# Attention on one core: one query block's scores of heads 1 to 13 made once and kept in SBUF, the maxima subtracted there by GpSimd

## The chip, the core and the metric

The kernel runs on one core of a Trainium2 chip. The core has a matrix engine (TensorE, "PE" in the profile, with its weight loads as "PEld"), a vector engine (DVE), a scalar engine for activation functions (ACT), GpSimd (POOL) and an engine that here issues DMAs (SP). Each runs its own list of instructions in order, and waits for the others through semaphores. SBUF is the on-chip memory that all of them use; matmuls write to PSUM, eight banks of 128 x 512 f32, from which DVE and ACT read. The metric is the time of one execution on the device in microseconds (us).

## The reference

A transformer block on 2048 tokens of width 448, all in f32:

```python
h = _layernorm(x) * (1 + ca) + sa            # ca, sa, ga, ... from silu(c) @ w_mod
q, k, v = heads(h @ wqkv)                    # 16 heads of 28
p = softmax(q @ k.T * 28 ** -0.5)            # 2048 x 2048 for each head
x = x + ga * (merge(p @ v) @ wo)
h = _layernorm(x) * (1 + cb) + sb
z = gelu(h @ w_in); z1, z2 = z[:, :896], _layernorm(z[:, 896:])
x = x + gb * ((z1 * (w_sp @ z2 + b_sp)) @ w_out)
```

The change is in the second and third of these lines' softmax. Everything behind it (the projection with `wo` and the gated MLP) is computed as before.

## The kernel before, in words

**Three stages.** The first 145 us make q, k and v (q and k are split into a high and a low part and go through DRAM to be stacked by head). The attention follows, to 864 us. The rest is the MLP, in which PE multiplies a combined form of `w_sp` whose block sums GpSimd has made during the attention.

**Scores are made twice.** The maximum of each query over all keys must be known before the exponential. For head h, `kst[h % 3]` and `qst[h % 3]` hold the stacked keys and queries, 128 rows x 2048. `m_mm` (PE L728) multiplies 128 queries by 512 keys into PSUM, queries on the partitions, and DVE takes the maximum along the keys (L733). That is 64 matmuls and 64 reductions a head. `m_max` then gathers them on DVE (L740) and negates and splits them on GpSimd (L742 to L143), `m_fin` transposes them on PE (L749), DVE copies them (L751), and two DMAs put them into rows 84 and 85 of `qst`, where `kst` has rows of ones. From then on every product of `kst` and `qst` has the query's maximum subtracted already. `s_mm` (PE L760) makes the scores a second time, now 128 keys by 512 queries, keys on the partitions; ACT takes the exponential out of PSUM into a tile `P` (L764), and `pv_mm` (PE L775) multiplies `V` by `P` into one PSUM bank for the whole head. A unit `u` is one key tile of 128 of one head: four `s_mm`, one for each block `qb` of 512 queries, and their exponentials. There are 256 units, 16 a head.

**What sets the order.** The schedule is written out by hand: the order in which the Python code issues is the order on each engine. The loop goes over units. In unit `u` it alternates the four `s_mm` of `u` with the four `m_mm` of unit `u + LEAD`, LEAD = 20, so that a head's maxima are ready when its exponentials start. After every second unit the products with `V` of the last two are issued. Other work is hung on slots (a slot is a unit's number) in two tables, `events` ahead of the unit and `late` behind it: the loading of a head's keys and queries (`load_head`, 30 slots ahead of the head), `m_max` and `m_fin` four slots ahead of it, the normalisation of the head before (`n_copy`, `n_sum`, `n_recip`, `n_bcast`, `n_mul`, `n_scatter`, at slots 1 to 9 of the next head), and on GpSimd the sums and differences of blocks of `w_sp` (`W_SUMS`, `ws_op`, slots 2 to 200; L882 adds or subtracts, L877 negates), whose blocks SP loads and stores in the same order. SP's list is in order too: a store waits there for the GpSimd operation ahead of it, and whatever stands behind waits with it.

**Buffers.** Seven PSUM banks serve scores and maxima; which of them a matmul gets is fixed when the program is written, by `First`, a small table of assumed times in units of one matmul. `P` has six tiles for two exponentials each. Two large SBUF areas that held the normed input of the first stage (`heapD0`, `heapD1`) and one that held the weights for q and k (`heapD2`) serve as the place of the attention's output `OT` and of the prepared `wo`.

## Time and profile before

| | |
|---|---|
| median of 3 runs (lowest to highest) | 1375.57 us (1374.93 to 1377.33) |
| span of the profiled execution, first to last instruction | 1375.3 us |
| busy over the span: PE, PEld, DVE, ACT, POOL | 1370.1, 973.9, 1069.3, 789.5, 356.1 us |
| granted TensorE clock | 1.000 |
| attention, first to last product with V | 150.9 to 863.5 us |

The span is what the profile shows of one execution, and it is 0.2 us from the median of the timed runs, so sums over the profile can be set against the median without a correction. "Busy" is the time in which at least one instruction of an engine was under way. PE's matmuls overlap, so PE counts as busy even where it goes from one matmul to the next more slowly than it could; for what one matmul costs, the distance from start to start is the thing to read. POOL's spans are rough.

### The profile page before, as it was taken

To read this page: it belongs to the slowest core of one execution; us is meant where nothing else is said; L and a number is where in the kernel's file an instruction comes from. 1 tells how busy PE (TensorE), PEld (TensorE's weight loads), DVE (VectorE), ACT (ScalarE), POOL (GpSimd) and SP (SyncE) were. 2 spreads that over 40 slices of the span, in tenths; PEclk is the share of its full clock that TensorE was granted. 3 is DMA by queue.
4 is the path that set the end of the run, shared out by engine and by line. 5 is a ranking of instruction groups with operands and counts; after the bars stand their busy time and mean duration, and the time that the engine had idled before them with its cause. 6 is when DMAs were issued, how large, how long until landed. Compare 5 with 4: busy or idle time off the path is not lost.

```text
span 1375.3 us, 20071 instructions
## 1 busy us (share of the span) xinstructions
PE 1370.1 (100%) x7088; PEld 973.9 (71%) x7088; DVE 1069.3 (78%) x1729; ACT 789.5 (57%) x1466; POOL 356.1 (26%) x358
## 2 busy tenths in 40 slices
PE   9999999999999999999999999999999999999998
PEld 8888655555555555555555554888898888888898
DVE  8898888888888888888888880662268798889682
ACT  6623666676767676767777779364234754444221
POOL 2144334243335544633442302200142000000000
PEclk9999999999999999999999999999999999999999
DMA  8464642455244534552343321533202433335842
GB/s 296 138 177 176 187 118 85 109 161 153 69 117 138 151 121 124 156 148 77 110 126 88 96 57 50 174 142 126 85 1 77 130 100 115 115 93 180 270 158 83
DMA packets 93345, 174.65 MB, mean 127 GB/s; under 512 B 17016, under 2 KB 32250, under 8 KB 90698
## 3 DMA queue, kind: packets, MB, share of 16 engines
q1 hardware_dynamic: 90526, 169.07, 40.9%
q10 hardware_dynamic: 2718, 4.30, 0.9%
q8 instruction: 56, 0.92, 0.3%
q14 instruction: 45, 0.37, 0.1%
HBM read 111.71 MB, written 56.82 MB: 123 GB/s over the span
## 4 chain that ended last, share of the span: by engine, by line
PE 97%; DVE 1%; ACT 0%; issue 0%; DMA 0%; POOL 0%; DVEq 0%; ACTq 0%
PE st_ps L760 19%; PE acc L1442 19%; PE o_ps L775 17%; PE mt L728 17%; PE z_ps L1334 5%; PE z_ps L1166 5%; PE pq L415 4%; PE wo_ps L1031 3%; PE y_ps L1522 2%; PE y_ps L1521 2%; PE y_ps L1520 2%; PE pv L397 2%; PE tp L193 1%; DVE st L368 0%; PE pv L554 0%
## 5 line engine op out<-in xcount | busy, mean ns | idle before, releaser
L733 DVE TENSOR_REDUCE pm<-mt 128x1 f32<-128x512 f32 x1024 | 631.3, 682 | 85.9 <-PE mt L728 85.8
L764 ACT ACTIVATE P<-st_ps 128x512 f32<-128x512 f32 x1024 | 514.4, 630 | 201.8 <-PE st_ps L760 201.8
L760 PE MATMUL st_ps<-qst,kst 128*128 128x512 f32 x1024 | 404.3, 406 | 0.0
L728 PE MATMUL mt<-kst,qst 128*128 128x512 f32 x1024 | 402.5, 393 | 0.1
L760 PEld LDWEIGHTS st_ps<-qst,kst 128*128 128x128 f32 x1024 | 191.2, 188 | 141.4 <-issue 93.1
L775 PE MATMUL o_ps<-P,V 128*32 128x512 f32 x2048 | 247.1, 598 | 0.0
L1442 PE MATMUL acc<-wsp_h,heapA 128*128 128x512 f32 x752 | 231.5, 389 | 0.0
L728 PEld LDWEIGHTS mt<-kst,qst 128*128 128x128 f32 x1024 | 192.4, 188 | 32.0 <-POOL kst L665 0.5
L882 POOL TENSOR_TENSOR ws_raw<-ws_raw 128x512 f32<-128x512 f32 x124 | 159.3, 1288 | 195.7 <-DMA ws_scr<-ws_raw 138.9
L1442 PEld LDWEIGHTS acc<-wsp_h,heapA 128*128 128x128 f32 x752 | 141.1, 188 | 29.2
L1442 PE MATMUL acc<-wsp_l,heapA 128*128 128x512 f32 x376 | 146.3, 389 | 0.0
L775 PEld LDWEIGHTS o_ps<-P,V 128*32 128x32 f32 x2048 | 54.7, 109 | 122.9 <-issue 114.6
L1222 ACT ACTIVATE wsp_h<-raw_sp 128x512 fp32r<-128x512 f32 x104 | 65.6, 632 | 125.7 <-PE acc L1442 111.2
L143 DVE TENSOR_TENSOR wsp_l<-raw_sp,wsp_h 128x512 fp32r<-128x512 f32 x104 | 70.4, 687 | 16.6 <-ACT wsp_h L1222 16.4
L1442 PEld LDWEIGHTS acc<-wsp_l,heapA 128*128 128x128 f32 x376 | 70.6, 188 | 14.7
L415 PE MATMUL pq<-heapD,heapD 128*128 128x512 f32 x196 | 61.8, 390 | 0.0
L1338 DVE BATCH_NORM_STATS2 stz<-z 128x6 f32<-128x448 f32 x32 | 19.9, 626 | 44.6 <-ACT z L1337 44.5
L143 DVE TENSOR_TENSOR heapA<-z,heapA 128x1536 fp32r<-128x1536 f32 (+2 forms) x25 | 39.9, 1605 | 6.6 <-ACT heapA L1257 6.5
L1337 ACT ACTIVATE z<-z_ps 128x448 f32<-128x448 f32 x32 | 17.4, 543 | 47.4 <-PE z_ps L1334 47.4
L415 PEld LDWEIGHTS pq<-heapD,heapD 128*128 128x128 f32 x196 | 36.7, 188 | 7.4
L804 POOL TENSOR_TENSOR osb<-osb,rb 128x512 f32<-128x512 f32 x15 | 19.3, 1287 | 85.6 <-DMA rb<-r_scr 80.8
L1521 PE MATMUL y_ps<-wouts,uT 128*128 128x448 f32 x112 | 40.9, 365 | 0.0
(231 smaller groups left out, 1432.1 us busy)
## 6 DMA issues: line engine op xcount, KB each, us to landing
ws_scr<-ws_raw SPq DMA_DIRECT2D x92, 256.0 KB
raw_sp<-ws_scr SPq DMA_DIRECT2D x92, 256.0 KB
ws_raw<-in_w_spT_dram SPq DMA_DIRECT2D x72, 256.0 KB
kst<-qk_scr SPq DMA_DIRECT2D x45, 224.0 KB
qst<-qk_scr SPq DMA_DIRECT2D x45, 224.0 KB
qk_scr<-qh SPq DMA_DIRECT2D x28, 256.0 KB
qk_scr<-ql SPq DMA_DIRECT2D x28, 256.0 KB
z_scr<-z1t SPq DMA_DIRECT2D x28, 256.0 KB
```

The lines of the kernel that those rows point to most:

```text
L143: eng.tensor_tensor(out=dst, in0=a, in1=hi.bitcast(F32), op=ALU.subtract)
L415: pe.matmul(pq, wqk[:, b, m * 128 : (m + 1) * 128], hT[g][:, a, :], start=j == 0, stop=j == NST - 1)
L728: pe.matmul(mt, qst[h % 3][:, t * 128 : (t + 1) * 128], kst[h % 3][:, kb * 512 : (kb + 1) * 512], start=True, stop=True)
L733: dve.tensor_reduce(out=pms[h][:, t, kb : kb + 1], in_=mt, axis=AX.X, op=ALU.max)
L760: pe.matmul(st, kst[h % 3][:, kt * 128 : (kt + 1) * 128], qst[h % 3][:, qb * 512 : (qb + 1) * 512], start=True, stop=True)
L764: act.activation(p, st, AF.Exp, scale=SCALE)
L775: pe.matmul(otile[h][32 * qb : 32 * qb + 32, :], V[:, kt, h, :], ptiles.pop((u, qb)), start=kt == 0, stop=kt == NT - 1)
L882: pool.tensor_tensor(out=ws_tile(op[0]), in0=ws_tile(op[2]), in1=ws_tile(op[4]), op=ALU.add if op[3] == "+" else ALU.subtract)
L1166: pe.matmul(ps_t, w1[:, b, f * 128 : (f + 1) * 128], h2T[g][:, a, :], start=j == 0, stop=j == NST - 1)
L1334: pe.matmul(ps_t[:, :D], h2T[g][:, a, tt * 128 : (tt + 1) * 128], w2[:, b, hf * D : (hf + 1) * D], start=j == 0, stop=j == NST - 1)
L1442: pe.matmul(a[j], z[:, c], w, start=start and k == 0, stop=st == 3 and k == 2, skip_group_check=not new or j == 3)
L1521: pe.matmul(y[:, :D], uT[k][:, 7 + f, ts], wouts[0][:, f, :], start=False, stop=False)
```

## The change

For heads 1 to 13 (`RAW`), the scores of query block 0 (queries 0 to 511) are made once.

* The 16 products of key tiles with these 512 queries (`r_mm`) are made at the place where the products for the maxima were made, 22 slots ahead, when rows 84 and 85 of `qst` are still zero. ACT copies each from PSUM to a tile in SBUF (`raw_tile`, a ring of 23 tiles in the areas `heapD0` and `heapD2` and 4 KB a partition of its own).
* DVE keeps an elementwise maximum over the 16 tiles (`r_max`, 15 operations a head, two inputs in SBUF). `r_turn` transposes the result in four pieces on PE, and DVE reduces it along the free axis into the first four columns of the maxima. The `m_mm` of these four query tiles (16 matmuls and 16 reductions a head) are gone.
* When the maxima stand in `qst`, `r_neg` multiplies a matrix with ones in rows 84 and 85 alone (`sel`, the tile `ones` written anew) by the 512 queries: each partition then has the negated maxima. ACT copies that to `rneg`.
* GpSimd adds `rneg` to each of the 16 raw tiles (`r_sub`), three slots or less ahead of the exponential, and ACT takes the exponential from SBUF (`x_exp`). The second product of these scores is gone.

Heads 0, 14 and 15 work as before. The loop now goes over pairs of units, and an order for PE is written as a string (`ORDERS`: s is a score, m a product for the maxima, r a raw score, p the products with V and the late events, | the events of the second unit). `P` has ten single tiles. Since the raw tiles use `heapD0` and `heapD2` up to slot 223, `OT` is laid out anew, and the splitting of the output (`o_split`) and the preparation of `wo` move behind slot 224.

```diff
-    ppool = att.enter_context(tc.tile_pool(name="ppool", bufs=6))
+    ppool = att.enter_context(tc.tile_pool(name="ppool", bufs=10))
+    rpool = att.enter_context(tc.tile_pool(name="rpool", bufs=1))
...
+            qb, o = divmod(c.start, 512)
+            i = (4 * b + qb) if b < 3 else (4 * b + qb - 12) if b < 6 else 12 + qb % 2
+            heap = heapD[int(3 <= b < 6 or b == 6 and qb < 2)]
+            return heap[p, i * 512 + o : i * 512 + o + c.stop - c.start]
...
+    def heap_turn():
+        heapD[0] = dpool.tile([128, 8 * 896], F32R, name="heapO", tag="heapD0")
+        heapD[2] = dpool.tile([128, 4 * 896], F32R, name="heapW", tag="heapD2")
+        wos.append(hview(heapD[2], 0, 8, D))
+
+    RAW = range(1, 14)
+    ring3 = []
+
+    def raw_tile(u):
+        if not ring3:
+            ring3.append(dpool.tile([128, 8 * 896], F32, name="rawA", tag="heapD0"))
+            ring3.append(dpool.tile([128, 4 * 896], F32, name="rawB", tag="heapD2"))
+            ring3.append(rpool.tile([128, 1024], F32, name="rawC"))
+        i = u % 23
+        t, i = (ring3[0], i) if i < 14 else (ring3[1], i - 14) if i < 21 else (ring3[2], i - 21)
+        return t[:, i * 512 : i * 512 + 512]
+
+    sel = ones.bitcast(F32R)
...
+        r = 4 if h in RAW else 0
+        if h not in mxv:
+            mxv[h] = npool.tile([128, NT], F32, name="mxv")
+        mx = mxv.pop(h)
+        dve.tensor_reduce(out=mx[:, r:], in_=pms.pop(h)[:, r:, :], axis=AX.X, op=ALU.max)
...
+    mxv, kept, rmax, rneg = {}, [], [], []
+
+    def score(name, h, kt, qb):
+        st = bank(name)
+        pe.matmul(st, kst[h % 3][:, kt * 128 : (kt + 1) * 128], qst[h % 3][:, qb * 512 : (qb + 1) * 512], start=True, stop=True)
+        return st
+
+    def r_mm(u):
+        act.activation(raw_tile(u), score("rt", *divmod(u, NT), 0), AF.Copy)
+        kept.append(u)
+
+    def r_max():
+        a = kept.pop(0)
+        if not rmax:
+            rmax.append(stage2.tile([128, 512], F32, name="rmax", tag="ql"))
+        first = raw_tile(kept.pop(0)) if a % NT == 0 else rmax[0]
+        spend("dve", 2.6)
+        dve.tensor_tensor(out=rmax[0], in0=raw_tile(a), in1=first, op=ALU.max)
+
+    def r_some(lag=1):
+        if len(kept) > lag + (len(kept) > 0 and kept[0] % NT == 0):
+            r_max()
+
+    def r_fin(h):
+        while kept and kept[0] < (h + 1) * NT:
+            r_max()
+
+    def r_turn(h):
+        tp = bank("rtp")
+        for t in range(4):
+            pe.transpose(tp[:, t * 128 : (t + 1) * 128], rmax[0][:, t * 128 : (t + 1) * 128], ident)
+        mxv[h] = npool.tile([128, NT], F32, name="mxv")
+        dve.tensor_reduce(out=mxv[h][:, 0:4], in_=tp.rearrange("p (a b) -> p a b", b=128), axis=AX.X, op=ALU.max)
+
+    def r_neg(h):
+        st = bank("rt")
+        pe.matmul(st, sel, qst[h % 3][:, 0:512], start=True, stop=True)
+        if not rneg:
+            rneg.append(stage2.tile([128, 512], F32, name="rneg", tag="ql"))
+        act.activation(rneg[0], st, AF.Copy)
+
+    def r_sub(u):
+        pool.tensor_tensor(out=raw_tile(u), in0=raw_tile(u), in1=rneg[0], op=ALU.add)
+
     ptiles = {}
 
+    def s_exp(u, qb, src):
+        p = ptiles[u, qb] = ppool.tile([128, 512], F32, name="P")
+        act.activation(p, src, AF.Exp, scale=SCALE)
+
     def s_mm(u, qb):
-        h, kt = divmod(u, NT)
-        st = bank("st_ps")
-        pe.matmul(st, kst[h % 3][:, kt * 128 : (kt + 1) * 128], qst[h % 3][:, qb * 512 : (qb + 1) * 512], start=True, stop=True)
-        if qb % 2 == 0:
-            ptiles[u, -1] = ppool.tile([128, 2, 512], F32, name="P")
-        p = ptiles[u, -1][:, qb % 2, :]
-        act.activation(p, st, AF.Exp, scale=SCALE)
-        ptiles[u, qb] = p
+        s_exp(u, qb, score("st_ps", *divmod(u, NT), qb))
+
+    def x_exp(u):
+        spend("st_ps", 2.1)
+        s_exp(u, 0, raw_tile(u))
...
+    for h in RAW:
+        at(h * NT - 6, r_fin, h)
+        at(h * NT - 6, r_turn, h, when=late)
+        at(h * NT - 1, r_neg, h)
+        for k in range(NT):
+            at(h * NT + (k // 2 - 1 if k < 4 else k - 3), r_sub, h * NT + k)
+    for c, slot in ((0, 226), (1, 230), (2, 236)):
         for qb in range(4):
-            at((hl + 1) * NT + (12 + qb if c == 2 else 18 + 2 * qb), o_split, c, qb)
+            at(slot + qb, o_split, c, qb)
...
+    at(224, heap_turn)
     for i in range(4):
-        at(120 + 8 * i, wo_load, i)
-        at(124 + 8 * i, wo_prep, i)
+        at(224 + 4 * i, wo_load, i)
+        at(228 + 4 * i, wo_prep, i)
...
+    pool.memset(ones[:, :], 0.0)
+    pool.memset(ones[64:86, :], 1.0)
+    pool.memset(ones[64:84, :], 0.0)
...
+    m_work, r_work = [[] for _ in range(NU + 2)], [[] for _ in range(NU + 2)]
+    for i in range(NT):
+        r_work[(0, 0, 1, 2, 2, 3, 4, 4, 5, 5, 6, 7, 7, 8, 9, 9)[i]].append(NT + i)
+    rest = [(j, kb) for j in range(NT + 8, 2 * NT) for kb in range(4)]
+    for u in range(12):
+        n = 4 - len(r_work[u])
+        m_work[u], rest = rest[:n], rest[n:]
+    assert not rest
+    for h in range(2, H):
+        t0 = 4 if h in RAW else 0
+        work = [(h * NT + t, kb) for t in range(t0, NT) for kb in range(4)]
+        for i in range(NT):
+            n = NT - t0
+            m_work[h * NT - LEAD + i] += work[i * n // 4 : (i + 1) * n // 4]
+            if t0:
+                r_work[h * NT - LEAD - 2 + i].append(h * NT + i)
...
+    ORDERS = {6: "mspm|rmssmsssmrm", 8: "mspmm|smsmsmsmsm"}
+
+    def pair(u):
+        ss = [[(v, qb) for qb in range(1 if v // NT in RAW else 0, 4)] if v < NU else [] for v in (u, u + 1)]
+        S_, M_, R_ = ss[0] + ss[1], m_work[u] + m_work[u + 1], r_work[u] + r_work[u + 1]
+        X_ = [v for v in (u, u + 1) if v < NU and v // NT in RAW]
+        xat = [4, 6] if u % NT == 0 else [1, 1]
...
+        for c in order + "s" * len(S_) + "r" * len(R_) + "m" * len(M_):
+            if c == "p":
+                if u > 0:
+                    pv_mm(u - 2)
+                    pv_mm(u - 1)
+                    first_free.pause(2)
+                run(late, u)
+            elif c == "|":
+                run(events, u + 1)
+            elif c == "s" and S_:
+                s_mm(*S_.pop(0))
+                n_o += 1
+                exps()
+            elif c == "r" and R_:
+                r_mm(R_.pop(0))
+                n_o += 1
+                exps()
+            elif c == "m" and M_:
+                m_mm(*M_.pop(0))
+                n_m += 1
+                if n_m % 2 == 0:
+                    r_some()
+        assert not X_
+        run(late, u + 1)
```

The change moves instructions at three places on which the prediction rests.

GpSimd (POOL), from one head's maxima to the next head's: `mxv` and `mxp` are the three small operations of `m_max`, `ws_raw` the block sums of `w_sp`, `osb` the normalisation of a head. Before:

```order
L742 TENSOR_SCALAR mxv<-mxv 128x16
L743 CAST mxp<-mxv 128x16
L143 TENSOR_TENSOR mxp<-mxv,mxp 128x16
L882 TENSOR_TENSOR ws_raw<-ws_raw 128x512 x9
L804 TENSOR_TENSOR osb<-osb,rb 128x512
L882 TENSOR_TENSOR ws_raw<-ws_raw 128x512 x2
L742 TENSOR_SCALAR mxv<-mxv 128x16
L743 CAST mxp<-mxv 128x16
```

and now, the first rows of the same head (`rawA`, `rawB` and `rawC` are raw tiles, `rneg` the negated maxima):

```order
L767 TENSOR_SCALAR mxv<-mxv 128x16
L768 CAST mxp<-mxv 128x16
L143 TENSOR_TENSOR mxp<-mxv,mxp 128x16
L822 TENSOR_TENSOR rawA<-rawA,rneg 128x512
L952 TENSOR_TENSOR ws_raw<-ws_raw 128x512 x2
L822 TENSOR_TENSOR rawA<-rawA,rneg 128x512 x2
L952 TENSOR_TENSOR ws_raw<-ws_raw 128x512
L822 TENSOR_TENSOR rawA<-rawA,rneg 128x512
L822 TENSOR_TENSOR rawB<-rawB,rneg 128x512
L952 TENSOR_TENSOR ws_raw<-ws_raw 128x512
L822 TENSOR_TENSOR rawB<-rawB,rneg 128x512 x2
L952 TENSOR_TENSOR ws_raw<-ws_raw 128x512
```

Between the block sums, which keep their order, stand 16 subtractions a head; a subtraction waits for the block sums ahead of it, and those for their DMAs.

TensorE (PE), a pair of units in the middle of a head. Before, from one group of products with V (`o_ps`) on, with scores (`st_ps`) and products for the maxima (`mt`) in turn, 16 to a pair:

```order
L775 MATMUL o_ps<-P,V 32x512 x8
L760 MATMUL st_ps<-qst_875,kst_874 128x512
L728 MATMUL mt<-kst_870,qst_871 128x512
L760 MATMUL st_ps<-qst_875,kst_874 128x512
L728 MATMUL mt<-kst_870,qst_871 128x512
L760 MATMUL st_ps<-qst_875,kst_874 128x512
L728 MATMUL mt<-kst_870,qst_871 128x512
L760 MATMUL st_ps<-qst_875,kst_874 128x512
L728 MATMUL mt<-kst_870,qst_871 128x512
L760 MATMUL st_ps<-qst_875,kst_874 128x512
```

and now, a whole pair (`rt` is a raw score; `kst_870` and `qst_871` are those of the head to come):

```order
L845 MATMUL o_ps<-P,V 32x512 x8
L750 MATMUL mt<-kst_870,qst_871 128x512
L784 MATMUL rt<-qst_871,kst_870 128x512
L750 MATMUL mt<-kst_870,qst_871 128x512
L784 MATMUL st_ps<-qst_875,kst_874 128x512 x2
L750 MATMUL mt<-kst_870,qst_871 128x512
L784 MATMUL st_ps<-qst_875,kst_874 128x512 x3
L750 MATMUL mt<-kst_870,qst_871 128x512
L784 MATMUL rt<-qst_871,kst_870 128x512
L750 MATMUL mt<-kst_870,qst_871 128x512 x2
L784 MATMUL st_ps<-qst_875,kst_874 128x512
```

Eight of one and eight of the other have become six scores, six products for the maxima and two raw scores.

The vector engine (DVE) and TensorE again, in the slots ahead of a head's maxima, where the running maximum is turned. On DVE there stood before (`pm` is a reduction, `osb` and `rt` belong to the normalisation of the head before):

```order
L784 COPY osb<-o_ps 128x512
L733 TENSOR_REDUCE pm<-mt 128x1 x12
L794 RECIPROCAL rt<-rt 128x16
L733 TENSOR_REDUCE pm<-mt 128x1 x32
L740 TENSOR_REDUCE mxv<-pm 128x16
L733 TENSOR_REDUCE pm<-mt 128x1 x4
L751 COPY nt<-mtp 32x128
```

and now, from six slots ahead of the head on (`rmax` is the running maximum, `rtp` its transpose, `mxv` the maxima by query):

```order
L797 TENSOR_TENSOR rmax<-rawB,rmax 128x512
L755 TENSOR_REDUCE pm<-mt 128x1 x2
L797 TENSOR_TENSOR rmax<-rawB,rmax 128x512
L797 TENSOR_TENSOR rmax<-rawC,rmax 128x512
L755 TENSOR_REDUCE pm<-mt 128x1
L812 TENSOR_REDUCE mxv<-rtp 128x4
L755 TENSOR_REDUCE pm<-mt 128x1 x5
L765 TENSOR_REDUCE mxv<-pm 128x12
L755 TENSOR_REDUCE pm<-mt 128x1
L776 COPY nt<-mtp 32x128
```

On PE, where before a score followed directly on the products with V as in the rows above, there is now:

```order
L784 MATMUL st_ps<-qst_873,kst_872 128x512
L845 MATMUL o_ps<-P,V 32x512 x8
L810 MATMUL rtp<-ident,rmax 128x128 x4
L750 MATMUL mt<-kst_874,qst_875 128x512
L784 MATMUL rt<-qst_871,kst_870 128x512
L750 MATMUL mt<-kst_874,qst_875 128x512
```

The transposes stand in PE's list behind the products with V and ahead of the next matmul, and they wait for the last of two operations on `rmax` that stand back to back on DVE.

61 lines of the change are left out of this document (35 added, 26 removed).

## The prediction, made before the changed kernel ran

> **What bounds the kernel now.** I read the page first, for the share of each engine and the chain that ended last.
>
> ```profile
> PE 1370.1 (100%) x7088; PEld 973.9 (71%) x7088; DVE 1069.3 (78%) x1729; ACT 789.5 (57%) x1466; POOL 356.1 (26%) x358
> PE 97%; DVE 1%; ACT 0%; issue 0%; DMA 0%; POOL 0%; DVEq 0%; ACTq 0%
> ```
>
> PE is busy throughout, and 97% of the chain is PE's. The shares are means over three stages, so the stage that changes has to be read by itself. The view by stretches, cut at the length of one head, gives it (columns: PE, PEld, DVE, ACT, POOL busy, then granted clock, DMA share, GB/s).
>
> ```profile
> 191.10:237.10 46.00, 46.00 (x261) 26.68 (x260) 40.20 (x69) 32.21 (x65) 16.30 (x16) 1.00 0.42 117
> 513.00:558.90 45.90, 45.90 (x258) 26.64 (x257) 40.16 (x70) 32.16 (x65) 24.91 (x24) 1.00 0.42 119
> 822.00:861.00 39.00, 39.00 (x244) 18.84 (x246) 2.51 (x7) 38.13 (x79) 9.33 (x12) 1.00 0.17 44
> ```
>
> A head takes 46.0 us; DVE works 40.2 of them, ACT 32.2, GpSimd 16 to 25. The clock is 1.00, so what is saved on PE is time. The timeline of one pair of units shows what sets the pace:
>
> ```profile
> 421.06 1.93 PE L775 MATMUL o_ps<-P,V 128*32 128x512 f32 x16
> 422.92 0.50 PE L760 MATMUL st_ps<-qst,kst 128*128 128x512 f32 x1
> 423.49 0.39 PE L760 MATMUL st_ps<-qst,kst 128*128 128x512 f32 x1
> 426.48 0.40 PE L728 MATMUL mt<-kst,qst 128*128 128x512 f32 x1
> 426.81 1.92 PE L775 MATMUL o_ps<-P,V 128*32 128x512 f32 x16
> 423.72 4.87 DVE L733 TENSOR_REDUCE pm<-mt 128x1 f32<-128x512 f32 x8
> 423.45 4.03 ACT L764 ACTIVATE P<-st_ps 128x512 f32<-128x512 f32 x8 [1.73 <-PE st_ps L760]
> ```
>
> A pair lasts 5.75 us (421.06 to 426.81). From 423.49 to 426.48 lie 13 matmuls, so one costs 0.230 us from start to start, not the 0.39 of its bar; 16 make 3.68, and the products with V with their gaps the other 2.07. ACT waits 1.73 us of each pair for PE; a reduction costs DVE 0.609, an exponential ACT 0.504. PE is the bound, and DVE is 0.87 behind it.
>
> **The change part by part.** PE loses 16 products a head: 16 x 0.230 = 3.68 us. It gains four transposes and one product (`r_neg`, 0.230). For transposes:
>
> ```profile
> 899.68 1.69 PE L193 MATMUL tp<-ident,x 128*128 128x128 f32 x14
> L193 PE MATMUL tp<-ident,x 128*128 128x128 f32 x42 | 5.1, 272 | 0.0
> ```
>
> (1.69 - 0.272) / 13 = 0.109 each, 0.44 for four. PE's own work is then 46.0 - 3.68 + 0.67 = 43.0 us a head. The raw scores only change their place: 13 heads x 16 of 1024.
>
> The other engines' new operations, by their nearest groups:
>
> ```profile
> L733 DVE TENSOR_REDUCE pm<-mt 128x1 f32<-128x512 f32 x1024 | 631.3, 682 | 85.9 <-PE mt L728 85.8
> L143 DVE TENSOR_TENSOR wsp_l<-raw_sp,wsp_h 128x512 fp32r<-128x512 f32 x104 | 70.4, 687 | 16.6 <-ACT wsp_h L1222 16.4
> L764 ACT ACTIVATE P<-st_ps 128x512 f32<-128x512 f32 x1024 | 514.4, 630 | 201.8 <-PE st_ps L760 201.8
> L1222 ACT ACTIVATE wsp_h<-raw_sp 128x512 fp32r<-128x512 f32 x104 | 65.6, 632 | 125.7 <-PE acc L1442 111.2 <-DMA raw_sp<-ws_scr 6.7 <-issue 5.1
> L882 POOL TENSOR_TENSOR ws_raw<-ws_raw 128x512 f32<-128x512 f32 x124 | 159.3, 1288 | 195.7 <-DMA ws_scr<-ws_raw 138.9 <-DMA ws_raw<-in_w_spT_dram 36.5 <-issue 13.7
> L877 POOL TENSOR_SCALAR ws_raw<-ws_raw 128x512 f32<-128x512 f32 x20 | 29.8, 1490 | 1.8
> L804 POOL TENSOR_TENSOR osb<-osb,rb 128x512 f32<-128x512 f32 x15 | 19.3, 1287 | 85.6 <-DMA rb<-r_scr 80.8 <-DVE pm L733 4.8
> ```
>
> DVE: 16 reductions of 682 ns go, and 15 maxima of two SBUF tiles (687) and one reduction of the transposes come: no change, 40.2 us a head. ACT: 16 copies and `rneg`, 17 x 0.504 = 8.6 more, 40.8; reading SBUF instead of PSUM costs nothing (632 against 630). GpSimd: 16 x 1.288 = 20.6 more. From one head's maxima to the next it then has, by the order of its instructions, 16 subtractions, one `osb`, 7 to 12 block sums and up to three negations. For heads 1 to 12 that is 36.4, 34.7, 41.8, 33.9, 36.0, 41.8, 35.1, 37.3, 40.5, 33.9, 34.7, 36.4 us, mean 36.9, where it had some 16. So all four engines would stand between 86% and 100% of 43 us, and what they do to each other decides.
>
> They meet at SBUF. Three places show an operation of DVE with two SBUF inputs beside GpSimd:
>
> ```profile
> 865.79 4.20 POOL L143 TENSOR_TENSOR heapA<-wraw,heapA 128x896 fp32r<-128x896 f32 x2 [1.37 <-ACT heapA L1110]
> 869.52 1.02 DVE L1126 TENSOR_TENSOR osb<-osb,rb 128x512 f32<-128x512 f32 x1
> 58.69 2.31 POOL L143 TENSOR_TENSOR acc_l<-acc,acc_h 128x448 fp32r<-128x448 f32 x2 [7.75 <-PE pv L397]
> 60.44 1.11 DVE L143 TENSOR_TENSOR heapD<-hfull,heapD 128x512 fp32r<-128x512 f32 x1 [1.57 <-ACT heapD L212]
> 1018.90 2.29 DVE L1247 TENSOR_TENSOR zt_sum<-z 128x2048 f32<-128x2048 f32 x1
> 1018.96 2.66 POOL L167 TENSOR_TENSOR rsz<-rsz,mhalf 128x1 f32<-128x1 f32 x1
> ```
>
> GpSimd ends at 869.99 and 61.00, and DVE 0.55 us behind it both times, with 1.02 and 1.11 us in place of 0.69: it stood until GpSimd was through. In the third, GpSimd began second and ended 0.43 us behind DVE. So `r_max` and whatever GpSimd runs exclude each other; the reductions out of PSUM run beside it at their usual 682. The Trainium skill has this as a rule that speaks against the change ("SBUF — State Buffer", section "Who interferes with whom"): a vector instruction with two SBUF inputs contends with a GpSimd instruction that reads SBUF, and the second to issue blocks until the first is through. The trace agrees, with the rows above; what it would make of the time is the second rival.
>
> The wait w of one `r_max` has the bounds 0 (GpSimd idle) and 1.29 us (a whole operation ahead of it). I take 0.2: when both are full, DVE comes to the next `r_max` two reductions (1.22 us) after the last, and GpSimd, let go by that one, is then at the end of its 1.29. DVE becomes 40.2 + 15 x 0.2 = 43.2, just covered by PE. GpSimd's loss to one `r_max` lies between 0 (it falls between two operations) and 0.69; I take 0.4, as in the third place, so 6 us a head.
>
> **Heads with many block sums.** For three heads GpSimd needs 41.8 + 6 = 47.8 (twice) and 46.5. It cannot fall far behind: `mtp` stands in PE's list and waits for `m_max` on GpSimd, and the exponentials of raw tiles stand in ACT's list ahead of those that free PSUM.
>
> **The turn of the maximum.** The last raw score is the last but one product of its pair, 0.46 us ahead of its end. ACT still has three exponentials ahead of it, then DVE two reductions and three `r_max`: 0.61 x 5 = 3.05 us, which I expect done 2.9 to 3.5 us into the next pair. PE gets to the transposes after 0.46 + 2.07 = 2.53. So PE waits 0.4 to 1.0 us a head; I take 0.7 (bounds 0, if DVE is ahead, and 1.6, if each of the three waits takes 0.4). With it the head is at 43.7.
>
> **GpSimd and its DMAs.** It waits in order for its stores and loads:
>
> ```profile
> POOL ws_raw L882 <- DMA ws_scr<-ws_raw: 138.9, 26, 15.5
> 511.12 2.67 POOL L882 TENSOR_TENSOR ws_raw<-ws_raw 128x512 f32<-128x512 f32 x2 [2.18 <-DMA ws_scr<-ws_raw]
> 527.17 2.66 POOL L882 TENSOR_TENSOR ws_raw<-ws_raw 128x512 f32<-128x512 f32 x2 [13.38 <-DMA ws_scr<-ws_raw]
> ```
>
> That cost nothing while it was early. Now subtractions stand behind such a sum. Most of the 13.4 us is filled, since about ten operations come ahead of that sum; I keep 1.5 us in the three full heads (bounds 0 and 5.8, rival three). The PSUM banks are dealt out by assumed times that know no w: no row prices that; between 0 and the 2.3 us that a head has left I take 0.4 for the ten lighter heads.
>
> What moves behind slot 224, 8 splits of the output (two operations each) and four preparations of `wo` (three), is at most 28 operations of the 1.29 us above, 36 us, on a GpSimd that is busy 9.33 of the 39 us in the last row of the second fence; that row is the last 20 units, and ahead of it lie 12 more at 5.75 us a pair, 34 us. It is hidden; without that cover the projection behind slot 256 would begin late by what is left over.
>
> The sum, against the span of 1375.3 us, 0.2 from the median: PE 13 x (-3.68 + 0.67) = -39.1; turns 13 x 0.7 = +9.1; the three full heads 47.8 - 43.7 twice and 46.5 - 43.7 = +11.0; their DMA waits +4.5; banks +4.0. Together -10.5, so **1365 us**.
>
> **The rivals.** First, *the full saving*: GpSimd and DVE slip past each other, no turn waits. -39.1, **1336 us**. For it: the reductions never meet GpSimd. Against it: the three places above.
>
> Second, *DVE becomes the bound* (slower): `r_max` comes at any point of an operation of GpSimd. Busy 36.9 of 47 us, half of 1.288 left on average: w = 0.51, and DVE needs 40.2 + 15 x 0.51 = 47.8 us a head, 1.8 more than before, 13 x 1.8 = +23.4: **1399 us**. It decides from w = (46.0 - 40.2) / 15 = 0.39 on. For it: nothing forces the two into step, since the products with V let DVE idle. Against: DVE that is late and GpSimd that is full do fall into step.
>
> Third, *late subtractions*: if half of the 138.9 us of waiting stays, 5.8 us in each of 12 heads, GpSimd needs 36.9 + 6 + 5.8 = 48.7, +2.7 x 12 = +32: **1407 us**. Against it: the wait was long because GpSimd was early.
>
> Fourth, *it comes out even*: the same terms with w near 0.38, **1375 us**. That the work is not removed is excluded: the order shows 816 products for maxima in place of 1024.
>
> **How the numbers follow.** The forecast (1345 to 1372) has 0.41, the full saving 0.11, even 0.13, DVE as the bound 0.21, late subtractions 0.14. Faster by over 0.2% (2.7 us, about what a measurement of this kernel tells from none) is 0.52, within it 0.13, slower 0.35. The range for 8 in 10 reaches from the full saving to the second and most of the third rival, 1336 to 1405; the forecast's own is 1345 to 1372.
>
> **What would show it.** In the changed kernel's profile: `r_max` near 0.9 us with the reductions still at 0.68 (w is right); near 1.2 or more, with PE's matmuls waiting for DVE, is the second rival. PE's transposes `rtp` should wait for DVE under 1 us each, 13 times. The stretches should be near 44 us for light heads and near 48 for those with many sums; if all are alike, GpSimd is not the limit. ACT's `x_exp` waiting for GpSimd behind a DMA is the third rival. The forecast is wrong if PE's chain is broken in every head.

## The result, and the profile after

The changed kernel takes **1448.31 us** (median of 4 runs, 1444.38 to 1453.03) against 1375.38 of the kernel before beside it: a ratio of 1.053 (95% interval 1.0506 to 1.0554). It is slower by 73 us, where 1365 was forecast; it lies outside the forecast's own range (1345 to 1372) and outside the wide one (1336 to 1405).

The page of the changed kernel, shares and chain:

```profile
PE 1384.0 (96%) x6945; PEld 945.5 (65%) x6945; DVE 1154.7 (80%) x1729; ACT 910.9 (63%) x1687; POOL 678.0 (47%) x569
PE 47%; DVE 10%; POOL 4%; issue 3%; DMA 2%; ACT 0%; SPq 0%; DVEq 0%; POOLq 0%
```

PE's share of the chain that ends last fell from 97% to 47%: PE is no longer busy without a break. DVE holds 10% of it now and GpSimd 4%.

Where the time went is read from the distance between the first product with V of one head and that of the next (worked out from the trace, not a view of it; us):

```text
head           0     1-12 (mean)   13     14     15
before        45.9     46.0       46.0   39.5   28.6
after         55.3     50.1       44.5   43.5   38.7
```

The span grew from 1375.3 to 1444.6, by 69.3: head 0 +9.4, heads 1 to 12 together +49, head 13 -1.5, heads 14 and 15 +4.0 and +10.1; the stages ahead of the attention and behind it give 1.7 back. So there are two losses. One is in the heads that make raw scores for a later one, 0 to 12. The other is in heads that were to work as before, 14 and 15, and head 0 has a part in this one too.

**The heads that make raw scores.** The view by stretches (columns: PE, PEld, DVE, ACT, POOL busy, granted clock, DMA share, GB/s), head 2, head 7, head 13 and the last one:

```profile
254.20:303.00 48.80, 46.05 (x249) 23.37 (x248) 47.31 (x69) 41.18 (x81) 41.14 (x32) 1.00 0.37 104
506.70:557.00 50.30, 46.74 (x249) 23.08 (x249) 49.05 (x69) 41.54 (x82) 42.70 (x33) 1.00 0.41 116
805.90:850.50 44.60, 43.76 (x247) 23.80 (x246) 40.22 (x69) 34.40 (x67) 38.04 (x40) 1.00 0.43 121
894.00:932.70 38.70, 38.70 (x183) 17.02 (x183) 0.48 (x2) 30.28 (x61) 2.90 (x3) 1.00 0.12 32
```

DVE has 69 instructions a head as before, and works 47.3 and 49.1 us on them in place of 40.2; it is busy 97% of these heads and PE is not. In head 13, which still subtracts but takes no maximum of raw scores for a later head, DVE is back at 40.2, and the head takes 44.5. The groups of instructions name the operation (busy us, mean ns of one):

```profile
L755 DVE TENSOR_REDUCE pm<-mt 128x1 f32<-128x512 f32 x816 | 520.3, 680 | 43.5 <-PE mt L750 43.1
L797 DVE TENSOR_TENSOR rmax<-rawA,rmax 128x512 f32<-128x512 f32 x110 | 120.0, 1091 | 1.2
L797 DVE TENSOR_TENSOR rmax<-rawB,rmax 128x512 f32<-128x512 f32 x56 | 65.3, 1166 | 0.4
L822 POOL TENSOR_TENSOR rawA<-rawA,rneg 128x512 f32<-128x512 f32 x126 | 181.9, 1460 | 11.1 <-ACT rneg L819 11.1
L952 POOL TENSOR_TENSOR ws_raw<-ws_raw 128x512 f32<-128x512 f32 x124 | 181.3, 1462 | 35.5 <-DMA ws_scr<-ws_raw 22.6
```

The reductions out of PSUM still take 680 ns. `r_max` takes 1.1 us (1115 ns over all 195), GpSimd's operations 1.46 in place of 1.29. The waits between 150 and 860 us (engine and line, released by what; us in all, times, longest):

```profile
PEld rtp L810 <- DVE rmax L797: 42.3, 13, 4.4
PEld mt L750 <- DVE pm L755: 38.9, 73, 1.1
PE rtp L810 <- DVE rmax L797: 30.5, 13, 3.5
PEld st_ps L784 <- DVE pm L755: 30.5, 64, 1.3
PEld mtp L774 <- POOL mxp L143: 16.0, 14, 3.1
ACT P L828 <- POOL rawA L822: 4.0, 2, 2.4
```

PE stands before the transposes (`rtp`) for `r_max`, once a head, 30.5 / 13 = 2.3 us on average; the other long waits are for banks that DVE has not read yet. ACT hardly ever waits for a subtraction. The timeline at the turn of one head, PE, DVE and GpSimd:

```profile
370.56 1.92 PE L845 MATMUL o_ps<-P,V 128*32 128x512 f32 x16
375.86 1.92 PE L845 MATMUL o_ps<-P,V 128*32 128x512 f32 x16
376.62 2.95 POOL L822 TENSOR_TENSOR rawA<-rawA,rneg 128x512 f32<-128x512 f32 x2
376.64 3.48 DVE L797 TENSOR_TENSOR rmax<-rawA,rmax 128x512 f32<-128x512 f32 x2
380.17 0.78 PE L810 MATMUL rtp<-ident,rmax 128*128 128x128 f32 x4 [2.39 <-DVE rmax L797]
380.61 0.78 PE L750 MATMUL mt<-kst,qst 128*128 128x512 f32 x1
381.18 0.63 PE L784 MATMUL rt<-qst,kst 128*128 128x512 f32 x1
381.61 0.63 PE L750 MATMUL mt<-kst,qst 128*128 128x512 f32 x1
385.55 0.64 PE L845 MATMUL o_ps<-P,V 128*32 128x512 f32 x4
```

The pair ahead of the turn lasts 5.30 us (370.56 to 375.86), as PE's work alone would have it. The pair with the turn lasts 9.69: two `r_max`, one behind the other, take 3.48 us between two subtractions, and PE waits 2.39 for them. Over heads 1 to 12 the fifth interval of a head, which has the turn, has a mean of 8.72 against 5.75 before; that alone is 3.0 of the 4.1 us that a head lost. Behind the stall the matmuls stand 0.43 us apart, not 0.23. The view by stretches says why: the granted clock is halved for a while.

```profile
370.50:375.80 5.30, 5.30 (x31) 2.97 (x30) 5.09 (x9) 4.40 (x10) 3.38 (x3) 1.00 0.24 78
377.20:380.10 2.90, 0.58 (x8) 0.00 (x0) 2.80 (x3) 1.09 (x3) 2.90 (x3) 1.00 0.09 20
380.60:383.90 3.30, 3.30 (x11) 2.62 (x9) 2.37 (x5) 1.68 (x3) 1.89 (x2) 0.50 0.24 84
```

**The last heads.** Timeline of a pair in head 15, where no raw scores are left, first in the kernel before and then in the changed one:

```profile
841.62 10.95 ACT L764 ACTIVATE P<-st_ps 128x512 f32<-128x512 f32 x22
843.97 2.11 PE L760 MATMUL st_ps<-qst,kst 128*128 128x512 f32 x8
846.01 1.92 PE L775 MATMUL o_ps<-P,V 128*32 128x512 f32 x16
847.87 2.14 PE L760 MATMUL st_ps<-qst,kst 128*128 128x512 f32 x8
```

```profile
897.13 2.11 PE L784 MATMUL st_ps<-qst,kst 128*128 128x512 f32 x8
897.73 4.03 ACT L828 ACTIVATE P<-st_ps 128x512 f32<-128x512 f32 x8 [1.14 <-PE st_ps L784]
899.17 3.19 PE L845 MATMUL o_ps<-P,V 128*32 128x512 f32 x16
902.29 2.11 PE L784 MATMUL st_ps<-qst,kst 128*128 128x512 f32 x8
```

A pair takes 5.16 us (897.13 to 902.29); it took 3.90 before (843.97 to 847.87). The products with V take 3.19 us where they took 1.92, and ACT, which had no gap, idles 1.14 in every pair. Each of the two waits for the other: from 894 to 933 us PE's weight loads for these products wait 10.3 us for ACT, and ACT 7.9 us for PE.

### The profile page after: what moved, and what is told of

It reads as the page before. It is cut to its first block, busy times and chain, and to the rows that moved or that the text cites. A ratio compares the mean times of both kernels' runs of the same rounds, so it can differ in the third digit from the quotient of the medians.

```text
span 1444.6 us, 20709 instructions
## 1 busy us (share of the span) xinstructions
PE 1384.0 (96%) x6945; PEld 945.5 (65%) x6945; DVE 1154.7 (80%) x1729; ACT 910.9 (63%) x1687; POOL 678.0 (47%) x569
## 4 chain that ended last, share of the span: by engine, by line
PE 47%; DVE 10%; POOL 4%; issue 3%; DMA 2%; ACT 0%; SPq 0%; DVEq 0%; POOLq 0%
PE acc L1591 18%; DVE pm L755 5%; PE o_ps L845 5%; PE z_ps L1483 5%; PE z_ps L1315 5%; DVE rmax L797 4%; PE st_ps L784 3%; PE mt L750 3%; PE wo_ps L1180 2%; PE y_ps L1670 2%; PE y_ps L1671 2%; PE y_ps L1669 2%; POOL rawB L822 1%; DMA rb<-r_scr 1%; POOL ws_raw L952 1%
## 5 line engine op out<-in xcount | busy, mean ns | idle before, releaser
L755 DVE TENSOR_REDUCE pm<-mt 128x1 f32<-128x512 f32 x816 | 520.3, 680 | 43.5 <-PE mt L750 43.1
L828 ACT ACTIVATE P<-st_ps 128x512 f32<-128x512 f32 x816 | 437.5, 620 | 57.3 <-PE st_ps L784 55.9
L750 PE MATMUL mt<-kst,qst 128*128 128x512 f32 x816 | 324.0, 420 | 9.2 <-DVE pm L755 8.6
L784 PE MATMUL st_ps<-qst,kst 128*128 128x512 f32 x816 | 284.0, 413 | 10.8 <-DVE pm L755 6.4
L952 POOL TENSOR_TENSOR ws_raw<-ws_raw 128x512 f32<-128x512 f32 x124 | 181.3, 1462 | 35.5 <-DMA ws_scr<-ws_raw 22.6
L822 POOL TENSOR_TENSOR rawA<-rawA,rneg 128x512 f32<-128x512 f32 x126 | 181.9, 1460 | 11.1 <-ACT rneg L819 11.1
L797 DVE TENSOR_TENSOR rmax<-rawA,rmax 128x512 f32<-128x512 f32 x110 | 120.0, 1091 | 1.2
L788 ACT ACTIVATE rawA<-rt 128x512 f32<-128x512 f32 x126 | 78.8, 626 | 49.0 <-PE rt L784 49.0
L822 POOL TENSOR_TENSOR rawB<-rawB,rneg 128x512 f32<-128x512 f32 x64 | 92.2, 1452 | 8.0 <-ACT rneg L819 8.0
L784 PE MATMUL rt<-qst,kst 128*128 128x512 f32 x208 | 83.2, 400 | 0.2 <-DVE pm L755 0.2
L828 ACT ACTIVATE P<-rawA 128x512 f32<-128x512 f32 x126 | 76.7, 663 | 4.0 <-POOL rawA L822 4.0
```

The source lines that it names most:

```text
L750: pe.matmul(mt, qst[h % 3][:, t * 128 : (t + 1) * 128], kst[h % 3][:, kb * 512 : (kb + 1) * 512], start=True, stop=True)
L755: dve.tensor_reduce(out=pms[h][:, t, kb : kb + 1], in_=mt, axis=AX.X, op=ALU.max)
L784: pe.matmul(st, kst[h % 3][:, kt * 128 : (kt + 1) * 128], qst[h % 3][:, qb * 512 : (qb + 1) * 512], start=True, stop=True)
L788: act.activation(raw_tile(u), score("rt", *divmod(u, NT), 0), AF.Copy)
L797: dve.tensor_tensor(out=rmax[0], in0=raw_tile(a), in1=first, op=ALU.max)
L822: pool.tensor_tensor(out=raw_tile(u), in0=raw_tile(u), in1=rneg[0], op=ALU.add)
```

## The experiments

The theory after this reading: GpSimd and `r_max` shut each other out of SBUF, so DVE becomes the bound, and two `r_max` in a row ahead of the turn stop PE (A). Against it stand these: the load of the engines alone is too much; the place of the turn in PE's list is what costs; what PE waits for is the `mtp` transpose, whose operands GpSimd makes behind its subtractions (B). The loss in heads 0, 14 and 15 should be one of order alone. All ratios are against the kernel before on the same chip (1375.4, 1375.9 and 1375.7 us in the three sets).

**Order in the heads without raw exponentials.** In such pairs the products with V went behind the first score; here they go behind all scores of the pair's first unit.

```diff
-  order += "s" * (i < len(ss[k])) + others[i : i + 1] + "p" * (k == 0 and i == 0)
+  order += "s" * (i < len(ss[k])) + others[i : i + 1]
+order += "p" * (k == 0)
```

> The changed kernel, but where a pair of units has no raw exponentials (heads 0, 14, 15) the products with V stand behind all scores of its first unit again, as before the change. Theory (the order of the last two heads costs by itself: there the products with V follow the pair's first score and wait for exponentials that ACT has not made): heads 14 and 15 go back from 43.5 and 38.7 us to 39.5 and 28.6, and the first pairs of head 0 from 6.5 towards 5.8; 14 to 17 us less than the changed kernel, about 1432 us. Rival (ACT or GpSimd is slower there for another reason): no change, 1446 to 1450.

Measured: 1429.63 us, ratio 1.0402 (1.0375 to 1.0428). Heads 14 and 15 are back at 39.5 and 28.6 us, head 0 falls from 55.3 to 51.8. Its timeline in head 15:

```profile
894.73 11.96 ACT L828 ACTIVATE P<-st_ps 128x512 f32<-128x512 f32 x24
894.75 1.92 PE L845 MATMUL o_ps<-P,V 128*32 128x512 f32 x16
896.60 2.11 PE L784 MATMUL st_ps<-qst,kst 128*128 128x512 f32 x8
898.64 1.92 PE L845 MATMUL o_ps<-P,V 128*32 128x512 f32 x16
```

ACT works without a gap again, and a pair takes 3.9 us. So 18.7 of the 73 us are this order and have nothing to do with raw scores. For head 0 the theory was only in part right: 5.9 us of its loss stay. It makes the raw scores of head 1, and its fifth interval, with the turn, is still 8.15 us. In pairs with raw exponentials the products with V also stand behind the first score, and undisturbed these pairs run at PE's pace (5.30 us above); there ACT has exponentials and copies that do not wait for that score.

**The maximum straight from PSUM.** `r_max` reads the raw score from its bank, directly behind ACT's copy, so it has one input in SBUF in place of two (the running maximum, or for the first of a head the tile before).

```diff
-act.activation(raw_tile(u), score("rt", *divmod(u, NT), 0), AF.Copy)
+st = score("rt", *divmod(u, NT), 0)
+act.activation(raw_tile(u), st, AF.Copy)
...
-dve.tensor_tensor(out=rmax[0], in0=raw_tile(a), in1=first, op=ALU.max)
+dve.tensor_tensor(out=rmax[0], in0=st, in1=raw_tile(u - 1) if u % NT == 1 else rmax[0], op=ALU.max)
```

> The changed kernel, but the running maximum reads the raw score out of its PSUM bank instead of the copy in SBUF: the same 195 operations on DVE with one SBUF input instead of two, made as soon as the score is there. Theory (DVE and GpSimd shut each other out of SBUF): the operation goes from 1.11 us to 0.69, GpSimd's subtraction from 1.46 to 1.29, the wait at the transposes from 3 us to under 1, heads 1 to 12 from 50.1 to 44 to 45.5 us: 60 to 70 us less, 1378 to 1388 us. Rival (the engines are simply too full, and the banks too few): the same load, and each bank is held longer, so 1435 to 1455.

Measured: 1432.47 us, 1.0412 (1.0397 to 1.0428). A miss on the time, which lies nearer to the rival's 1435 to 1455 than to the theory's 1378 to 1388: heads 1 to 12 came down from 50.1 to 48.6, not to 45. The groups of this kernel, DVE and GpSimd:

```profile
L794 DVE TENSOR_TENSOR rmax<-rt,rmax 128x512 f32<-128x512 f32 x182 | 125.5, 690 | 70.7 <-ACT rawA L789 42.8 <-ACT rawB L789 22.2 <-ACT rawC L789 5.5
L827 POOL TENSOR_TENSOR rawA<-rawA,rneg 128x512 f32<-128x512 f32 x126 | 160.5, 1291 | 14.0 <-ACT rneg L824 14.0
```

The exclusion is gone: 690 and 1291 ns, where operations of these kinds took 687 and 1288 before the change. But DVE now idles 70.7 us ahead of these maxima, for ACT's copy out of the same bank. One wait was exchanged for another, and from this run alone the load could as well have been the cause. The Trainium skill ("PSUM — Partial Sum Buffer", section "PSUM bank collisions raise a hardware error") has it that two engines that read one bank in the same partitions at the same time collide. In this program they do not meet, since the second reader waits for the first: all 195 maxima of this run begin 0.03 us or more behind the end of ACT's copy.

**The turn later.** `r_turn` one slot later, everything else as in the changed kernel.

```diff
-at(h * NT - 6, r_turn, h, when=late)
+at(h * NT - 5, r_turn, h, when=late)
```

> The changed kernel, but the transposes of the running maximum stand at the end of their pair of units instead of behind its products with V, 2.7 us of PE's work later. If only their place costs (PE waits there 3.4 us more than in other pairs, 13 times): about 44 us less, 1404. If the exclusion at SBUF is the cause, what is late is DVE, and it is late for the matmuls' banks too: 10 to 25 us less, 1423 to 1438.

Measured: 1439.12 us, 1.0471 (1.043 to 1.0512). The fifth interval falls from 8.72 to 7.68 us on average, heads 1 to 12 from 50.1 to 49.3. The place of the turn is worth some 9 us, a rough figure, since the four runs lie between 1434.6 and 1449.0; the exclusion as the cause was to give 1423 to 1438, which is just missed. The place is not the main cause: it was to bring 44 us if it were, and the interval is still 2.4 above an undisturbed pair.

**The first two together.**

> The maximum from PSUM and the order of heads 0, 14 and 15 as before, together. Theory: the two savings add, 75 to 85 us less than the changed kernel, 1363 to 1373 us, so slightly faster than the kernel before the change. Rival (load): 1420 or more.

Measured: 1422.39 us, 1.034 (1.0323 to 1.0358). Heads 14 and 15 are at 39.5 and 28.8, but heads 1 to 12 at 48.6 as with the second edit alone, so the forecast of this run was missed as well; the time is where the rival, load, had put it (1420 or more). In the waiting that is left at PE the lines for `mtp` have grown, from 16.0 and 3.9 us in the changed kernel:

```profile
PEld mtp L774 <- POOL mxp L143: 28.7, 13, 2.9
PE mtp L774 <- POOL mxp L143: 16.8, 12, 2.0
```

That is B, which grew when the long wait for `r_max` at the turn went. It is not the longest wait: PE's loads for scores wait 47.2 us for banks that `r_max` has yet to read, which this edit itself brought.

**The maximum from PSUM, one reduction later.** As the run before, but each maximum stands in DVE's list behind the next reduction (`r_some` takes from `kept` after every `m_mm`), so that ACT has more time for its copy; the bank is held until then.

```diff
 act.activation(raw_tile(u), st, AF.Copy)
-if u % NT:
-    first_free.also()
-    dve.tensor_tensor(out=rmax[0], in0=st, in1=raw_tile(u - 1) if u % NT == 1 else rmax[0], op=ALU.max)
+if u % NT:
+    kept.append((u, st, first_free.hold()))
...
 m_mm(*M_.pop(0))
 n_m += 1
-if n_m % 2 == 0:
-    r_some()
+r_some()
```

> As the run with both edits (maximum from PSUM, order of heads 0, 14 and 15 as before: 1422 us), but each maximum stands on DVE behind the next reduction, since in that run DVE waited 70 us for ACT's copy of the same score. Theory A (that wait was the experiment's own, and the exclusion at SBUF is most of what is left): the pairs in the middle of a head go from 5.68 to 5.3 us, heads 1 to 12 from 48.7 to 46 us, 1385 to 1395 us. Theory B (DVE is late at the two turns of a head's maxima, whoever it waits for, and PE stands there): the wait at the transposes of the maxima (pair 6 of a head, 7.2 us) stays, 1395 to 1410 us. Theory C (the banks are too few): no gain, 1420 or more.

Measured: 1394.85 us, 1.0138 (1.0123 to 1.0153). Group and waits:

```profile
L798 DVE TENSOR_TENSOR rmax<-rt,rmax 128x512 f32<-128x512 f32 x182 | 125.0, 687 | 29.9 <-ACT rawA L789 18.8 <-ACT rawB L789 8.5 <-ACT rawC L789 2.2
PEld mtp L774 <- POOL mxp L143: 26.2, 14, 3.9
PE mtp L774 <- POOL mxp L143: 13.5, 12, 3.0
```

Most heads take 46.2 us, those with many block sums 49.8, 51.0 and 47.5 (3, 6, 9). Against the first run, which differs by the source and the place of the maxima and by the banks, which are dealt out anew, this is 35 us less with the same number of operations on each engine: load alone falls as the cause. Source and place went together here; `r_max` from SBUF at this place was not run. The middle pairs are at 5.46 us, the turn at 5.8; the sixth interval, in which `mtp` comes, is at 6.5 in light heads and up to 10.0. So both A and B hold.

**No subtraction.** The changed kernel without GpSimd's 208 subtractions. The raw tiles go to the exponential with scale 0, so the softmax of the first query block in heads 1 to 13 is left out of what is computed.

```diff
-pool.tensor_tensor(out=raw_tile(u), in0=raw_tile(u), in1=rneg[0], op=ALU.add)
+pass
...
-s_exp(u, 0, raw_tile(u))
+s_exp(u, 0, raw_tile(u), 0.0)
```

> The changed kernel without GpSimd's 208 subtractions; the exponentials of the raw tiles are taken with scale 0, so that block 0 of heads 1 to 13 is left out of what is computed (its attention is a plain mean). Theory A (exclusion between GpSimd and DVE): GpSimd is left with its block sums, about 40% of the time, the maximum goes from 1.11 to about 0.9 us, and the changed kernel's 1448 falls to 1405 to 1420 us. Theory B (DVE's queue is late at the turns): the waits at the turns stay but for that, 1420 to 1435. If GpSimd's late subtractions were the cause, the time falls to 1385 or less.

Measured: 1387.91 us, 1.0097 (1.0078 to 1.0115), 60 less than the changed kernel. Both theories had expected more time than that (1405 to 1435), and 1385 or less was to mean that the subtractions came too late.

```profile
L797 DVE TENSOR_TENSOR rmax<-rawA,rmax 128x512 f32<-128x512 f32 x110 | 84.5, 769 | 1.2
PEld rtp L810 <- DVE rmax L797: 23.8, 13, 4.4
POOL ws_raw L952 <- DMA ws_scr<-ws_raw: 141.9, 24, 16.4
```

Heads 1 to 12 take 44.9 us, 1.1 less than before the change, and `r_max` 786 ns on average: what is left of its waiting comes from the block sums. Heads 0, 14 and 15 are as slow as in the changed kernel (57.0, 43.5, 38.7), so the two losses are separate. GpSimd has its slack back: its wait for stores is 141.9 us, where it was 138.9 before the change and 22.6 with it. That subtractions come too late for ACT is not what is saved: in the changed kernel ACT waits 6.2 us for raw tiles in all. The maxima stand where they stood in the changed kernel, so their place alone is not what costs heads 1 to 12. How much of the 60 us is exclusion and how much the wait for `mxp` behind subtractions this run cannot say by itself; the next two bear on it.

**The maxima made two slots earlier.** On top of the run with the maxima from PSUM one reduction later: the reductions of heads 3 and up two slots earlier, `m_max` one, so GpSimd has longer for its three small operations. Then the same with `r_max` still from SBUF, on top of the order of the first run.

```diff
-m_work[h * NT - LEAD + i] += work[i * n // 4 : (i + 1) * n // 4]
+m_work[h * NT - LEAD - (2 if h > 2 else 0) + i] += work[i * n // 4 : (i + 1) * n // 4]
...
-at(h * NT + NT - LEAD, m_max, h)
+at(h * NT + NT - LEAD - (1 if h > 2 else 0), m_max, h)
```

> As the first run of this call, but the products for the maxima of heads 3 to 15 are made two slots earlier and the gathering of the maxima stands one slot earlier, so that DVE and GpSimd have 2.5 us more for it before PE comes to the transpose of the maxima. Theory B: pair 6 of a head falls from 7.2 to under 5.8 us and the two pairs behind it with it, 25 to 40 us less than the first run, 1355 to 1375 us. Theory A or C: no change against the first run within 8 us.

> The changed kernel with the order of heads 0, 14 and 15 as before (1430 us) and the earlier products and gathering of the run above, with the maximum still from SBUF. Theory B: the wait at the transposes of the maxima is gone (20 us in the changed kernel), but not the one at the running maximum's, 1410 to 1420 us. Theory A: the time stays within 1422 to 1435 us, since the stall is at the running maximum.

Measured: 1383.5 us, 1.0056 (1.0041 to 1.0071), with the maxima from PSUM; 1419.49, 1.0316 (1.0297 to 1.0336), with those from SBUF. The early maxima alone are worth 11 us in the one case and 10 in the other; the source of `r_max`, with its place, is worth 36. B had been given 25 to 40 us in the first case, so it is real and smaller; in the second its 1410 to 1420 was just met. In the latter kernel the fifth interval is still 8.1 us and `r_max` 1062 ns. With the former, PE's loads for `mtp` wait 5.8 us for `mxp` in the whole attention, in place of 26.2, and most heads take 45.6 us, 0.4 less than before the change:

```profile
PEld mtp L774 <- POOL mxp L143: 5.8, 4, 2.6
PE mtp L774 <- POOL mxp L143: 2.3, 2, 1.7
```

It still loses in head 0 (51.2), head 1 (49.5) and head 6 (48.1).

**Towards a faster version: raw scores from head 2 on, and the small operations on DVE.** On top of that kernel, head 1 as before the change (first run), `m_max`'s three operations of 128 x 16 on DVE in place of GpSimd (second), and both.

```diff
-RAW = range(1, 14)
+RAW = range(2, 14)
```

```diff
-pool.tensor_scalar(out=mx, in0=mx, scalar1=-1.0, scalar2=None, op0=ALU.mult)
-pool.tensor_copy(mxs[h][:, 0, :], mx)
-sub(pool, mxs[h][:, 1, :], mx, mxs[h][:, 0, :])
+dve.tensor_scalar(out=mx, in0=mx, scalar1=-1.0, scalar2=None, op0=ALU.mult)
+dve.tensor_copy(mxs[h][:, 0, :], mx)
+sub(dve, mxs[h][:, 1, :], mx, mxs[h][:, 0, :])
```

> Heads 2 to 13 alone keep raw scores, head 1 is as in the kernel before; everything else as in y3_psum_and_early_maxima (1383.5 us). That run still lost 5.2 us in head 0 (51.2 against 46.0) and 3.5 in head 1 (49.5). If this is the making of head 1's raw scores beside head 0's full 64 exponentials in ten slots, head 0 goes back to about 46.0 and head 1, whose slots then make head 2's raw scores over sixteen slots, to 46 to 48; one head's saving (0.4 us) is given up: 1376 to 1380 us. Rival: the loss belongs to the head in which the extra scores of the first lead are made, whichever it is, and only moves to head 1: 1382 to 1386 us.

> y3_psum_and_early_maxima, with the three small operations on a head's maxima (times -1, the rounded copy, the difference) on DVE instead of GpSimd. If what is left in the fifth interval (5.93 us against 5.46 in the middle ones, and 7.9 in head 1) is these operations standing in GpSimd's queue behind subtractions of 1.29 us, the fifth interval falls to 5.5 to 5.6 in heads 2 to 12 and below 7 in head 1, the wait for mxp is gone: 1374 to 1379 us. Rival: the fifth interval is long because of the reductions on DVE (the turned maxima and pm) in any case: 1381 to 1385 us.

> z1 and z3 together. If both readings hold: heads 2 to 12 at 45.1 to 45.4, head 0 at 46.0, head 1 below 47: 1368 to 1375 us, no slower than the kernel before and at best 0.5% faster. If either falls, 1376 to 1382 us.

Measured: 1382.02 us, 1.0046 (1.0032 to 1.006), for the first. Head 0 falls to 48.7 and head 1 rises to 50.9; the rival was right (1382 to 1386), the loss moves with the first raw head. The other two went far wrong: 1415.84, 1.0311 (1.0289 to 1.0332), and 1415.14, 1.0283 (1.0263 to 1.0303). They are slower by 32 and 33 us than without the second edit, though GpSimd's queue no longer holds the small operations. The timeline of the second kernel at one turn shows what was overlooked, GpSimd first, then DVE and PE:

```profile
468.79 2.55 POOL L822 TENSOR_TENSOR rawB<-rawB,rneg 128x512 f32<-128x512 f32 x2
471.26 1.29 POOL L952 TENSOR_TENSOR ws_raw<-ws_raw 128x512 f32<-128x512 f32 x1
469.94 0.19 DVE L767 TENSOR_SCALAR mxv<-mxv 128x16 f32<-128x16 f32 x1
470.17 1.21 DVE L768 CAST mxp<-mxv 128x16 fp32r<-128x16 f32 x1
471.41 1.18 DVE L143 TENSOR_TENSOR mxp<-mxv,mxp 128x16 fp32r<-128x16 f32 x1
473.25 0.80 PE L784 MATMUL rt<-qst,kst 128*128 128x512 f32 x1 [2.46 <-DVE pm L755]
```

The first of the three, begun as the first subtraction was ending, took 0.19 us for 16 elements a partition. The second ends at 471.38, just behind the second subtraction (471.34), and the third at 472.59, just behind the block sum (472.55). Each tiny operation took a whole one of GpSimd, the reductions behind them came 2.4 us late, and PE stopped for a bank. Over the attention PE's raw scores (`rt`) wait 23.0 us for such reductions, ten times; without the second edit they never do. This is exclusion without any load: two operations on 16 columns. It also goes further than the prediction had it, since the second has a single SBUF input. The Trainium skill ("SBUF — State Buffer", section "Who interferes with whom") says that too: copies, casts and `tensor_scalar` can, under conditions on their operands, contend for the shared pair of ports as well. The trace agrees, with the 1.21 us above.

No version here beats the kernel before. The best, 1382.0, is 0.46% behind it.

## Why the prediction was wrong

**PE's own work: right for a pair.** 43.0 us a head was said; undisturbed pairs take 5.30, and 8 x 5.30 with the 0.67 of transposes and `r_neg` is 43.1. No run shows a whole head at that: head 13 takes 44.5, and without subtractions heads 1 to 12 take 44.9.

**The wait w of one `r_max`: the step that failed.** I had named the exclusion, its rows and the point (0.39 us) from which DVE becomes the bound, and then took 0.2, on the argument that DVE late and GpSimd full "do fall into step". That did not help. Measured: 1115 ns against the 687 of the same operation with its score from PSUM, w = 0.43. With this the prediction's own formula gives DVE 40.2 + 15 x 0.43 = 46.7 us a head, and the stretches show 47.3 and 49.1. The argument took the rhythm of two reductions, then one `r_max`, and it fails in that rhythm. 89 of the 195 come so in the changed kernel's trace, at 1.19 us on average (counted in the trace, not a view of it). 22 met no operation of GpSimd and ran free. 52 met one that had begun under 0.13 us earlier, and 35 of these waited all of it out and took 1.81 us. The other 15 met an older one. So the two do meet in step, but `r_max` comes as GpSimd's next operation begins: a GpSimd that is full leaves no gap behind the one that ends. In the list `r_max` also come two or more in a row, one such row ahead of each turn. In 9 of the 12 rows of heads 1 to 12 the second took 1.56 us or more, behind an operation of GpSimd that had begun before the first was through.

**The turn: the largest mis-sized term.** 0.7 us of waiting a head was said, 1.6 as the bound. PE waits 2.3 on average at `rtp`, and the interval is 3.4 longer than an undisturbed pair. The last `r_max` ahead of the transposes are such rows of two, and in 7 of 12 both waited, 3.0 to 3.4 us for what takes 1.4 alone; so a mean was applied here where a wait is near its bound twice. The bound of 1.6 itself was wrong: it took three waits of 0.4 each, where one wait can be 1.1 (the longest `r_max` took 1.83 us) and the prediction's own bound for one was 1.29.

**The clock: no term.** Five times in the attention, behind stalls at the turn, the clock is 0.50 for 3.41 us; that is some 1.7 us each, 8 to 9 in all (an estimate, half of 5 x 3.41). The clock was read as 1.00 and taken as given, but it held only as long as PE had no gap. Where the stalls went, so did the spells: four with the turn later, none in the attention with the maxima from PSUM and made early.

**Heads 0, 14 and 15: no term.** The sum has 13 heads. That the new order string changes pairs without raw exponentials too stood in the order of PE's instructions, and no term was made of it. By the first experiment it is 18.7 us, a quarter of the whole loss.

**The small operations for `mtp`: not named as a wait.** That `mtp` waits for `m_max` on GpSimd was said, as a reason why GpSimd cannot fall behind; that the three small operations queue behind subtractions of 1.29 us was not priced. Moving them ahead saved 10 and 11 us.

**What held.** The reductions stayed at 680 ns. GpSimd's loss to one `r_max` was taken as 0.4; it is 0.32: in heads 1 to 12 the operations on 128 x 512 take 4.8 us a head more than 1.288 each, over 15 `r_max`. GpSimd is not the limit: 41 to 43 us of 49 to 50. Heads 3, 6 and 9 are longer than their neighbours, by 2.0 us on average (51.6 against 49.6) where 3.7, and 1.5 for their stores, were said. The late subtractions (third rival) are excluded: ACT waited 6.2 us for raw tiles in all. What moved behind slot 224 is hidden: behind the last product with V the rest takes 511.9 us, 512.4 before. The cost of dealing the banks (0.4 a head) cannot be told apart in these traces.

**The rivals.** The second, DVE as the bound, is what happened in heads 1 to 12, with the mark it was given: `r_max` near 1.2 us (1.115) and matmuls that wait for DVE. It was priced at 1.8 us a head by DVE's work alone. Measured 4.1: the stall at the turn comes on top, and so does the slow clock behind it. With the order in the other heads, which no rival had, the time passed even the highest of them, 1407.

By the runs, the 73 us of loss are: order in the heads without raw exponentials 19; source and place of `r_max` (exclusion, with the stalls and most of the slow clock that it causes) 35; the small operations behind subtractions 11. After these 65 the kernel (1383.5) is still 8 us behind the one before, and its heads 0, 1 and 6 together lie 10.8 us over 46.0. From there to the full saving of the first rival (1336) it is 47 us, most of it in the ordinary heads, which take 45.6 us and not 43.0; no run told this apart further.

## What to carry to other kernels

Before work is moved to GpSimd, list every DVE operation that would run beside it and ask which touch SBUF with two inputs, or are copies and casts within SBUF: each can cost a whole operation of GpSimd however small it is, and two in a row cost it twice. A bound of a wait is what one meets at the worst place on PE's path, not the mean of many places. When an order is rewritten, look at the stretches that the change does not mean to touch: here they cost a quarter of the loss and came back with one line.
